# A mask built by VectorE instead of GpSimd, and a new list of steps, in a fused attention and feed-forward kernel

## The chip, the cores and the metric

The kernel runs on one core of one Trainium2 chip. A core has five engines with queues of their own: TensorE (PE) multiplies matrices, VectorE (DVE), ScalarE (ACT) and GpSimd (POOL) work on elements, and SyncE (SP) issues the DMAs. Each engine takes its instructions strictly in the order of its queue and waits at the head of it for semaphores of the others. The metric is the device time of one execution in microseconds; lower is better.

## The reference

For each of 32 heads (4 batches, 8 heads, head size 48, 768 time steps) a matrix state is decayed by a complex number per row, receives an outer product, and is read by the query. The 384 values of a token then pass a feed-forward layer with a gate.

```
mag = sqrt(a_re^2 + a_im^2);  scale = min(mag, 0.999) / (mag + 1e-6)
a_re_n, a_im_n = a_re*scale, a_im*scale
for t in range(768):
    new_re = a_re_n[t]*S_re - a_im_n[t]*S_im
    new_im = a_re_n[t]*S_im + a_im_n[t]*S_re
    S_re, S_im = new_re + outer(k[t], v[t]), new_im
    y[t] = q[t] @ S_re
x = y as (3072 tokens, 384);  h = x @ w_in (384 x 2048)
out = (h * sigmoid(1.702*h)) @ w_out (2048 x 384)
```

## The kernel before

The recurrence is done in chunks. The 3072 tokens are 12 units of 256 time steps, each of two chunks of 128. For a unit, `prepare` turns the decays into running products (scans on VectorE) and angles (logarithms, exponentials, arctangent, sine and cosine on ScalarE, whose function tables are reloaded between the kinds), and multiplies queries and keys by them: the last two multiplications are the rotations `rot0` (into tile `qr`) and `rot1` (in place in `qk`), line 231. The first unit is prepared in two halves of 128 steps, so that TensorE can start earlier. `remap` (L452 to L456) then copies the rotated data with ten DMAs per half into `qkh`, where the features of a head lie on the partitions. `attend` computes scores (L517), multiplies them by the causal mask (L523, result `pm`), turns the keys (L536), forms the new state (L561) and blends scores and state into the attention output (L507).

`moe` is the feed-forward layer. Its steps are a hidden product (L657), two SiLU passes on ScalarE (L669, L671) with a difference on VectorE (L673, `gl`), and an output product (L686). The units fall into seven groups; the first has one unit and works with whole fp32 weights (`valA0` to `valA7` of w_in, `valU0` to `valU7` of w_out), the others with weights split in a high and a low half (`hiA`, `loA`, ...). The weights arrive as 64-bit words. A weight tile is converted by four instructions: L249, L252 and L256 on VectorE and L255 on ScalarE; later it is split by L269 (ScalarE) and L274 (VectorE). Lines 718 to 743 check the ranges of weights and angles.

The mask has four blocks of 128 columns. Block 0 is made by a memset and an affine select; blocks 1 to 3 are block 0 with its four quarters of 32 partitions rotated, which takes twelve copies of 32 partitions x 128 columns (L160).

Every step of `prepare`, `attend`, `moe` and the conversions is entered in a `Plan` by `add`, with its engine and with what it reads and writes. The 1736 steps are then issued in the order of a table of numbers, `ORDER`, which sets the order in every engine's queue. The instructions ahead of the plan (constants, mask) are placed by the framework. Twenty products with the identity (L434, `WARM = 20`), whose result nobody reads, are steps as well; they wait for the first half's `rot1` and stand between TensorE's first steps. They write a bank that the first hidden product overwrites.

Of the kernel before, what the change touches and what calls it, by code (L numbers as in the profile page):

```python
# [16 lines left out]
ALU = mybir.AluOpType  # L17
# [78 lines left out]
def attention_moe(ctx: ExitStack, tc: tile.TileContext, qk_in, v, a_in, w_in, w_out, qn, kn, vn, an, bn, out):  # L96
# [49 lines left out]
    nc.vector.memset(b_hpi, HALF_PI)  # L146
    make_identity(nc, ident)
    nc.gpsimd.memset(mask, 1.0)
    nc.gpsimd.memset(runs, 1)
    run_of = {T: runs[:, 0 : NR * (T + 1)], L: runs[:, NR * (T + 1) :]}  # L150
    for n, x in run_of.items():
        nc.gpsimd.memset(x.rearrange("p (r t) -> p r t", t=n + 1)[:, :, 0], 0)
    nc.gpsimd.affine_select(
        out=mask[:, 0, :], in_=mask[:, 0, :], pattern=[[1, P]], compare_op=ALU.is_ge,
        fill=0.0, base=0, channel_multiplier=-1,
    )
    for j in range(1, 4):
        for g in range(4):
            o = (g + j) % 4
            nc.gpsimd.tensor_copy(out=mask[o * QL : (o + 1) * QL, j, :], in_=mask[g * QL : (g + 1) * QL, 0, :])  # L160
# [986 lines left out]
```

## Time and profile before

| | before |
|---|---|
| median of 3 runs | 550.34 us (550.18 to 550.40) |
| profiled execution | 550.39 us |
| its span in the trace | 548.7 us |
| TensorE busy | 521.2 us (95%) |
| VectorE busy | 391.1 us (71%) |
| ScalarE busy | 368.7 us (67%) |
| GpSimd busy | 12.3 us (2%) |

The span is what the trace covers; the time around it belongs to starting and ending the program. A busy engine is one with an instruction under way: two instructions of one engine overlap by some hundredths of a microsecond, so the time that one costs its queue is read from the start of the next.

### The profile page before, as it was taken

What the parts mean: (1) busy time and instruction counts of PE and PEld (TensorE: products, weight loads), DVE (VectorE), ACT (ScalarE), POOL (GpSimd) and SP (SyncE); (2) the same over time, 40 slices, a digit from 0 to 9 for tenths busy, and PEclk for the clock granted to TensorE, in tenths of its full rate; (3) what the DMA queues carried; (4) which work ended last, traced back from release to release, by engine and by line L of the source; (5) the groups of instructions that cost most, each with busy time, mean ns of one, the idle gap of its engine ahead of it and who ended that gap; (6) DMA issues with size and microseconds to landing.
All of it is one profiled execution on the core that took longest, in us unless ns stands there. A gap on an engine that the chain in (4) does not pass through costs nothing.

```text
span 548.7 us, 14354 instructions
## 1 busy us (share of the span) xinstructions
PE 521.2 (95%) x6122; PEld 446.9 (81%) x6122; DVE 391.1 (71%) x625; ACT 368.7 (67%) x559; POOL 12.3 (2%) x55
## 2 busy tenths in 40 slices
PE   0399999999999999999999999999999999999997
PEld 0389988999988888888888888888888888888885
DVE  7999999999979989987766844856366535421142
ACT  7898989979699988688795679248665242132221
POOL 7000000000000000000000000000000000000000
PEclk9999999999999999999999999999999999999999
DMA  8859963626576668868237427445441162100121
GB/s 344 284 191 354 252 258 89 206 54 156 201 181 202 151 197 206 236 168 252 74 92 228 68 65 174 145 133 117 136 134 49 50 145 91 62 15 34 39 87 61
DMA packets 29253, 82.02 MB, mean 149 GB/s; under 512 B 4096, under 2 KB 7168, under 8 KB 29184
## 3 DMA queue, kind: packets, MB, share of 16 engines
q1 hardware_dynamic: 29184, 81.06, 50.5%
q8 instruction: 49, 0.80, 0.6%
q14 instruction: 20, 0.16, 0.1%
HBM read 57.41 MB, written 4.72 MB: 113 GB/s over the span
## 4 chain that ended last, share of the span: by engine, by line
PE 89%; DVE 8%; DMA 1%; issue 1%; ACT 1%; SPq 0%; DVEq 0%
PE o_ps L686 36%; PE h_ps L657 36%; PE x_ps L507 7%; PE z_ps L561 3%; PE z_ps L517 3%; PE p_ps L517 2%; DVE qk L231 1%; PE p_ps L536 1%; PE z_ps L536 1%; DMA raw<-in_w_in_dram 1%; DVE s L231 1%; DVE valA L256 1%; DVE qr L231 1%; DVE valU L252 0%; DMA qkh<-qk 0%
## 5 line engine op out<-in xcount | busy, mean ns | idle before, releaser
L669 ACT ACTIVATE gh<-h_ps 128x512 fp32r<-128x512 f32 x88 | 52.4, 596 | 108.2 <-PE h_ps L657 76.5
L673 DVE TENSOR_TENSOR gl<-h_ps,gh 128x512 fp32r<-128x512 f32 x88 | 60.3, 687 | 85.3 <-ACT h_ps L671 74.0
L657 PE MATMUL h_ps<-xhi,hiA 128*128 128x512 f32 (+1 forms) x288 | 108.9, 378 | 0.4 <-DVE gl L673 0.4
L657 PE MATMUL h_ps<-xhi,loA 128*128 128x512 f32 (+1 forms) x288 | 107.1, 372 | 0.0
L657 PE MATMUL h_ps<-xlo,hiA 128*128 128x512 f32 (+1 forms) x288 | 107.0, 372 | 0.0
L686 PE MATMUL o_ps<-gh,hiU 128*128 128x512 f32 (+1 forms) x288 | 79.7, 377 | 0.0
L686 PE MATMUL o_ps<-gl,hiU 128*128 128x512 f32 (+1 forms) x288 | 79.4, 376 | 0.0
L686 PE MATMUL o_ps<-gh,loU 128*128 128x512 f32 (+1 forms) x288 | 78.2, 372 | 0.0
L890 ACT ACT_TABLE_LOAD x56 | 71.8, 1283 | 1.8 <-PEq L1135 0.9
L657 PEld LDWEIGHTS h_ps<-xhi,hiA 128*128 128x128 f32 x288 | 54.2, 188 | 10.6 <-DVE gl L673 0.9
L657 PEld LDWEIGHTS h_ps<-xhi,loA 128*128 128x128 f32 x288 | 54.2, 188 | 9.6
L657 PEld LDWEIGHTS h_ps<-xlo,hiA 128*128 128x128 f32 x288 | 54.3, 188 | 9.0
L686 PEld LDWEIGHTS o_ps<-gh,loU 128*128 128x128 f32 x288 | 52.3, 188 | 9.5
L686 PEld LDWEIGHTS o_ps<-gh,hiU 128*128 128x128 f32 x288 | 51.4, 188 | 9.9 <-ACT gh L669 0.5
L686 PEld LDWEIGHTS o_ps<-gl,hiU 128*128 128x128 f32 x288 | 51.5, 188 | 9.6 <-issue 0.4
L671 ACT ACTIVATE h_ps<-h_ps 128x512 f32<-128x512 f32 x88 | 51.8, 592 | 0.0
L231 DVE TENSOR_TENSOR qk<-qk,s 128x768 f32<-128x768 f32 (+2 forms) x39 | 44.0, 1134 | 0.8 <-ACT s L427 0.5
L507 PE MATMUL x_ps<-pm,v 128*32 128x128 f32 x768 | 39.4, 274 | 0.0
L723 DVE TENSOR_REDUCE fit<-raw_w 128x1 f32<-128x384 f32 x64 | 33.5, 544 | 5.4 <-DMA raw_w<-in_w_out_dram 4.4
L507 PE MATMUL x_ps<-qkh,st 96*32 96x128 f32 x640 | 34.0, 272 | 0.0
L434 PE MATMUL h_ps<-qk,ident 128*128 128x256 f32 x40 | 11.9, 460 | 22.2 <-DVE qk L231 22.2
L434 PEld LDWEIGHTS h_ps<-qk,ident 128*128 128x128 f32 x40 | 9.2, 237 | 23.8 <-issue 22.2
(104 smaller groups left out, 791.2 us busy)
## 6 DMA issues: line engine op xcount, KB each, us to landing
v<-in_v_dram SPq DMA_DIRECT2D x24, 416.0 KB, 4.4
ri<-in_a_dram SPq DMA_DIRECT2D x11, 768.0 KB, 5.9
qk<-in_qk_dram SPq DMA_DIRECT2D x11, 768.0 KB, 6.4
qkh<-qr SPq DMA_DIRECT2D x22, 288.6 KB, 5.8
qkh<-qk SPq DMA_DIRECT2D x22, 288.6 KB, 4.8
raw<-in_w_in_dram SPq DMA_DIRECT2D x8, 768.0 KB, 7.1
raw<-in_w_out_dram SPq DMA_DIRECT2D x8, 768.0 KB, 7.4
raw_w<-in_w_in_dram SPq DMA_DIRECT2D x16, 384.0 KB, 3.3
```

Source lines behind the costliest of these rows:

```text
L231: add(en, t, rank, lambda: e.tensor_tensor(out=out, in0=a, in1=b, op=alu), **kw)
L434: add("PE", 0.43, -WARM + k, lambda k=k, dst=dst: mm(h_ps[0][:, k % 2 * T : (k % 2 + 1) * T], lhsT=ident, rhs=dst[:, k % NR, 0:T], start=T ...
L507: mm(x_ps[32 * j : 32 * j + 32, r, :], lhsT=lt, rhs=rt, start=n == 0, stop=n == len(steps) - 1)
L517: mm(ps_[to : to + QL, j, lo:L], lhsT=at(h, 1, c)[:, lo : lo + QL], rhs=at(h, 0, c)[:, lo:L], start=True, stop=True)
L561: mm(z_ps[g * QL : (g + 1) * QL, h * D : h * D + D], lhsT=kt[h // 4][:, h % 4, g * QL : (g + 1) * QL], rhs=vt[:, lo : lo + D], start=True, ...
L657: mm(h_ps[hb][:, k * n_x : (k + 1) * n_x], lhsT=ww[:, r * T + f * P : r * T + (f + 1) * P], rhs=x[:, r, xs], start=n == 0, stop=n == last)
L669: add("ACT", a_t(CW) - 0.13, rk(order_), lambda hb=hb, gb=gb: act(out=high.g(gb), in_=h_ps[hb], func=AF.Silu, scale=SLOPE), r=[f"h{hb}"], ...
L671: add("ACT", a_t(CW) - 0.13, rk(order_), lambda hb=hb: act(out=h_ps[hb], in_=h_ps[hb], func=AF.Silu, scale=SLOPE), w=[f"h{hb}"], tab=SILU, ...
L673: add("DVE", d_t(CW), rk(order_), lambda hb=hb, gb=gb: dve.tensor_tensor(out=glo[gb], in0=h_ps[hb], in1=high.g(gb).bitcast(F32), op=ALU.su ...
L686: mm(o_ps[c][:, xs], lhsT=y[:, f * DM + c * P : f * DM + (c + 1) * P], rhs=x[:, k * n_x : (k + 1) * n_x], start=begins and k == 0 and n == ...
L723: add("DVE", d_t(CK), rk + 2, lambda x=x, op=op: dve.tensor_reduce(out=f_w[:, x, n : n + 1], in_=weights.looked_at()[:, :, 1], op=op, axis ...
L890: nc.scalar.preload_act_table_set(o[5])
```

## The change

The twelve copies of the mask are issued to VectorE, and block 0 of the mask is made first on GpSimd, ahead of the identity matrix and of the other constants; its memset covers 128 columns in place of 512. `ORDER` holds the same 1736 steps in another order, which concerns all engines from the first load to the last output. The steps themselves are the same.

```diff
+    nc.gpsimd.memset(mask[:, 0, :], 1.0)
+    nc.gpsimd.affine_select(
+        out=mask[:, 0, :], in_=mask[:, 0, :], pattern=[[1, P]], compare_op=ALU.is_ge,
+        fill=0.0, base=0, channel_multiplier=-1,
+    )
     make_identity(nc, ident)
-    nc.gpsimd.memset(mask, 1.0)
     nc.gpsimd.memset(runs, 1)
...
-    nc.gpsimd.affine_select(
-        out=mask[:, 0, :], in_=mask[:, 0, :], pattern=[[1, P]], compare_op=ALU.is_ge,
-        fill=0.0, base=0, channel_multiplier=-1,
-    )
     for j in range(1, 4):
         for g in range(4):
             o = (g + j) % 4
-            nc.gpsimd.tensor_copy(out=mask[o * QL : (o + 1) * QL, j, :], in_=mask[g * QL : (g + 1) * QL, 0, :])
+            nc.vector.tensor_copy(out=mask[o * QL : (o + 1) * QL, j, :], in_=mask[g * QL : (g + 1) * QL, 0, :])
...
 ORDER = """
-80 0 137 5 15 20 100 25 81 82 84 83 85 86 1 3 2 87 94 139 4 138 88 103
```

On VectorE's queue, in the first unit's first half (`s0` to `s4` are its work tiles), the instructions behind the first ratio stood so before:

```order
L231 TENSOR_TENSOR s1_84<-ri_80,s3_86 128x3x128
L256 ISA valA0_159<-raw0_72,valA0_159 128x1536
L231 TENSOR_TENSOR s1_84<-s0_83,s1_84 128x3x128
L249 TENSOR_SCALAR valA1_173<-raw1_73 128x768
L339 TENSOR_SCALAR s0_83<-s0_83 128x3x128
L252 SCALAR_TENSOR_TENSOR valA1_173<-raw1_73,valA1_173 128x768
L358 SCALAR_TENSOR_TENSOR s3_86<-s0_83,s2_85 128x129 x3
L231 TENSOR_TENSOR s1_84<-ri_80,s3_86 128x3x128
```

and stand so now:

```order
L231 TENSOR_TENSOR s1_84<-ri_80,s3_86 128x3x128
L160 COPY mask_64<-mask_64 32x128 x12
L249 TENSOR_SCALAR valA1_166<-raw1_73 128x768
L339 TENSOR_SCALAR s0_83<-s0_83 128x3x128
L252 SCALAR_TENSOR_TENSOR valA1_166<-raw1_73,valA1_166 128x768
L256 ISA valA0_158<-raw0_72,valA0_158 128x1536
L231 TENSOR_TENSOR s1_84<-s0_83,s1_84 128x3x128
L358 SCALAR_TENSOR_TENSOR s3_86<-s0_83,s2_85 128x129 x3
L231 TENSOR_TENSOR s1_84<-ri_80,s3_86 128x3x128
```

The twelve copies stand behind the first half's ratio (the first row), and the last conversion step of `valA0` (L256) and the second half's sum (the next L231) have moved behind the conversion of `valA1`.

On TensorE's queue the first instructions were:

```order
L434 MATMUL h_ps0_107<-qk_81,ident_63 128x256 x13
L536 MATMUL o_ps0_109<-ident_63,qkh0_78 128x96 x4
L517 MATMUL p_ps_104<-qkh0_78 32x128 x4
L517 MATMUL p_ps_104<-qkh0_78 32x96 x4
L517 MATMUL p_ps_104<-qkh0_78 32x64 x4
L517 MATMUL p_ps_104<-qkh0_78 32x32 x4
L517 MATMUL z_ps_105<-qkh0_78 32x128 x4
L517 MATMUL z_ps_105<-qkh0_78 32x96 x4
L517 MATMUL z_ps_105<-qkh0_78 32x64 x4
L517 MATMUL z_ps_105<-qkh0_78 32x32 x4
L434 MATMUL h_ps0_107<-qk_81,ident_63 128x256 x5
L536 MATMUL o_ps1_110<-ident_63,qkh0_78 128x96 x4
```

and are:

```order
L434 MATMUL h_ps0_107<-qk_81,ident_63 128x256 x11
L536 MATMUL o_ps0_109<-ident_63,qkh0_78 128x96 x4
L434 MATMUL h_ps0_107<-qk_81,ident_63 128x256
L517 MATMUL z_ps_105<-qkh0_78 32x128 x4
L517 MATMUL z_ps_105<-qkh0_78 32x96 x4
L517 MATMUL z_ps_105<-qkh0_78 32x64 x4
L517 MATMUL z_ps_105<-qkh0_78 32x32 x4
L517 MATMUL p_ps_104<-qkh0_78 32x128 x4
L517 MATMUL p_ps_104<-qkh0_78 32x96 x4
L517 MATMUL p_ps_104<-qkh0_78 32x64 x4
L517 MATMUL p_ps_104<-qkh0_78 32x32 x4
L536 MATMUL o_ps1_110<-ident_63,qkh0_78 128x96 x4
```

Eleven instead of thirteen of the products with the identity stand ahead of the first useful one; one stands behind it, the two halves of the scores have changed places, and the five ahead of the second key turn are gone from there. Both queues hold all twenty of them ahead of the first hidden product or between the steps up to it.

On VectorE's queue the last two conversions of w_out, `valU6` and `valU7`, had this between them:

```order
L256 ISA valU6_893<-raw2_74,valU6_893 128x1536
L571 TENSOR_TENSOR xlo1_94<-x_ps_106,xhi1_886 128x3x128
L231 TENSOR_TENSOR qk_81<-qk_81,s3_86 128x3x256
L523 TENSOR_TENSOR pm1_98<-z_ps_105,mask_64 128x512
L231 TENSOR_TENSOR qk_81<-qk_81,s2_85 128x3x256
L249 TENSOR_SCALAR valU7_945<-raw3_75 128x768
L231 TENSOR_TENSOR qr_82<-qk_81,s0_83 128x3x512
L252 SCALAR_TENSOR_TENSOR valU7_945<-raw3_75,valU7_945 128x768
L231 TENSOR_TENSOR s1_84<-s3_86,s1_84 128x3x256
L274 TENSOR_TENSOR loA0_1012<-valA0_159,hiA0_226 128x768
L256 ISA valU7_945<-raw3_75,valU7_945 128x1536
```

and have now:

```order
L256 ISA valU6_835<-raw2_74,valU6_835 128x1536
L523 TENSOR_TENSOR pm1_98<-z_ps_105,mask_64 128x512
L523 TENSOR_TENSOR pm0_97<-p_ps_104,mask_64 128x512
L231 TENSOR_TENSOR qk_81<-qk_81,s2_85 128x3x256
L571 TENSOR_TENSOR xlo1_94<-x_ps_106,xhi1_935 128x3x128
L252 SCALAR_TENSOR_TENSOR valU7_858<-raw3_75,valU7_858 128x768
L231 TENSOR_TENSOR qr_82<-qk_81,s0_83 128x3x512
L256 ISA valU7_858<-raw3_75,valU7_858 128x1536
```

The split of `valA0` (L274) and the next unit's sum no longer stand between the two, and two mask products do.

## Rows read from the trace of the kernel before

**Rows 1.** The page, part 1: busy us, share of the span and instructions of each engine

```profile
PE 521.2 (95%) x6122; PEld 446.9 (81%) x6122; DVE 391.1 (71%) x625; ACT 368.7 (67%) x559; POOL 12.3 (2%) x55
```

**Rows 2.** Waits of TensorE over the span: us in total, times, longest

```profile
PE h_ps L434 <- DVE qk L231: 22.2, 1, 22.2
PE z_ps L561 <- DVE pm L523: 0.8, 1, 0.8
PE h_ps L657 <- DVE gl L673: 0.4, 1, 0.4
```

**Rows 3.** TensorE in time: start us, us, line, tiles, records, idle before and releaser

```profile
22.21 8.38 PE L434 MATMUL h_ps<-qk,ident 128*128 128x256 f32 x26 [22.21 <-DVE qk L231]
30.43 0.49 PE L536 MATMUL o_ps<-ident,qkh 96*128 96x96 f32 x4
...
32.10 2.43 PE L434 MATMUL h_ps<-qk,ident 128*128 128x256 f32 x10
...
37.45 0.84 PE L561 MATMUL z_ps<-v,kt 128*32 128x48 f32 x46 [0.78 <-DVE pm L523]
...
39.92 2.94 PE L657 MATMUL h_ps<-x,valA 128*128 128x128 f32 x24
...
86.16 1.56 PE L657 MATMUL h_ps<-x,valA 128*128 128x256 f32 x6
87.56 0.49 PE L536 MATMUL p_ps<-ident,qkh 96*128 96x96 f32 x4
...
88.22 1.49 PE L686 MATMUL o_ps<-g,valU 128*128 128x256 f32 x6
...
92.21 4.18 PE L686 MATMUL o_ps<-g,valU 128*128 128x256 f32 x18
96.05 0.47 PE L657 MATMUL h_ps<-xhi,hiA 128*128 128x256 f32 x1
```

**Rows 4.** Busy us in stretches: PE, PEld, DVE, ACT, POOL, PEclk, DMA share, GB/s

```profile
10.00:20.00 10.00, 0.00 (x0) 0.00 (x0) 9.96 (x24) 8.65 (x16) 0.99 (x6) 1.00 1.03 412
...
90.00:100.00 10.00, 10.00 (x152) 9.22 (x142) 9.96 (x15) 9.56 (x12) 0.00 (x0) 1.00 0.71 150
```

**Rows 5.** Tile valU, 84 to 97 us: duration ns, starts; idle us caused, times

```profile
L256 DVE CUSTOM_DVE_ANT_0 valU<-raw,valU x2: 948/948/949, 83.9 to 92.5; 128x1536 uint16<-128x1536 uint16 x2
...
  DVE valU L256: 0.2, 1
```

**Rows 6.** VectorE in time, columns as for TensorE above

```profile
5.19 0.56 DVE L231 TENSOR_TENSOR s<-s,s 128x384 f32<-128x384 f32 x1 [2.40 <-ACT s L207]
...
7.66 0.64 DVE L231 TENSOR_TENSOR s<-ri,s 128x384 f32<-128x384 f32 x1
8.23 1.04 DVE L256 CUSTOM_DVE_ANT_0 valA<-raw,valA 128x1536 uint16<-128x1536 uint16 x1
...
10.32 0.77 DVE L339 TENSOR_SCALAR s<-s 128x384 f32<-128x384 f32 x1
...
12.84 0.53 DVE L231 TENSOR_TENSOR s<-ri,s 128x384 f32<-128x384 f32 x1
13.29 0.15 DVE L366 TENSOR_SCALAR small<-s 128x3 f32<-128x3 f32 x1
...
13.57 0.53 DVE L249 TENSOR_SCALAR valA<-raw 128x768 int32<-128x768 int32 x1
14.02 0.42 DVE L339 TENSOR_SCALAR s<-s 128x384 f32<-128x384 f32 x1
...
15.49 0.53 DVE L231 TENSOR_TENSOR qk<-qk,s 128x384 f32<-128x384 f32 x1
...
21.15 0.96 DVE L231 TENSOR_TENSOR qk<-qk,s 128x768 f32<-128x768 f32 x1
...
36.61 0.69 DVE L523 TENSOR_TENSOR pm<-z_ps,mask 128x512 f32<-128x512 f32 x1
```

**Rows 7.** GpSimd in time, 3 to 11 us

```profile
3.64 6.34 POOL L160 COPY mask<-mask 32x128 bf16<-32x128 bf16 x12
```

145 rows, old and new, of the table ORDER are left out of this document.

## The prediction

> **What bounds the kernel now.** I read the page's busy shares first: TensorE is busy for 521.2 of 548.7 us [rows 1]. The waits of TensorE come next [rows 2]: one of 22.2 us ahead of its first instruction, one of 0.8 and one of 0.4. The rest of its idle time lies behind its last product. From 22 us on the kernel is a TensorE queue that hardly ever stops, so a change that adds and removes no useful product can gain at the start, at those two waits, and nowhere else; it can lose anywhere.
>
> The start is read from TensorE in time [rows 3]. The first thing that it does, at 22.21, is the run of 26 records of identity products (13 products, two records each). They do no useful work; the first useful product is at 30.43, and another run of them at 32.10 is one of two that stand between useful steps (14 records in all). They wait for VectorE's `rot1`, which starts at 21.15 and takes 0.96 [rows 6]. So `rot1` sets when TensorE's queue starts, and the fillers, twenty before and after, only shift with it.
>
> VectorE sets `rot1`: it is busy for 9.96 of the 10 us from 10 to 20 [rows 4], so whatever is put ahead of `rot1` on its queue delays it. It stays the second bound up to about 96 us: from 90 to 100 it is busy 9.96 of 10 us, and the tile `valU7`, ready at 92.5 + 0.95 = 93.45, made TensorE's weight load wait 0.2 us [rows 4, 5]. TensorE then starts the second group's first hidden product at 96.05 [rows 3]. Behind that TensorE waited for VectorE once more, 0.4 us at L657 [rows 2].
>
> **The change part by part.** *The copies.* VectorE is idle for 2.40 us ahead of 5.19, where it waits for ScalarE's squares [rows 6]. By the order of its queue the copies do not run there: they stand behind the ratio (7.66 before), in the stretch without idle time. The queue is in order, so all twelve are paid by `rot1`. The trace has no such copy on VectorE. From below: an operation on 3 columns takes 0.15 us and hides 0.08 of it under its neighbour (12.84 + 0.53 = 13.37 against a start at 13.29), net 0.07, twelve of them 0.84. From above: one on 384 fp32 columns takes 0.42, twelve of them 5.0 [rows 6]. At 128 columns the straight line between the two is 0.15 + 0.27 x 125/381 = 0.24, less 0.08 = 0.16; the elements are half as long, so I take 0.13, or 1.56 us.
>
> [...]
>
> *What GpSimd gives back.* Its twelve copies ran from 3.64 for 6.34 us [rows 7]. In that time VectorE was slower than later on the same shapes [rows 6]: L231 0.64 against 0.53, twice; L256 1.04 against 0.95 [rows 5]; L339 0.77 against 0.42. That is 0.11 + 0.11 + 0.09 + 0.35 = 0.66 us, which `rot1` gets back. GpSimd's queue has little else that anybody needs early.
>
> [...]
>
> *The new order ahead of `rot1`.* The same instructions stand ahead of it in both, but for one more L249 (five weight tiles begun, not four). That is 14.02 - 13.57 = 0.45 us [rows 6]. SP now puts one more weight of 768 KB ahead of the first load of `qk`. At 412 GB/s [rows 4] that is 1.9 us; its first user stood at 15.49 [rows 6] and stands some four instructions later, so this is hidden. Without that cover it would cost up to 1.9.
>
> `rot1` therefore ends 1.56 + 0.45 - 0.66 = 1.35 us later, and TensorE's queue with it.
>
> *What TensorE gets back.* The wait of 0.78 us at 37.45 [rows 3] was for `pm`, whose second half VectorE did at 36.61 [rows 6], behind five conversion steps. In the new queue both halves of `pm` follow the second half's `rot1` directly. Five fillers stand behind the blend, so the hidden products' input is ready too. I take the 0.78 as gone. What is late next is the second half: its `rot1` has moved back behind two conversions and a sum, about 2.6 us at 0.87 each. TensorE asks for it later as well: six hidden products now stand ahead of the second chunk's scores.
>
> *The conversions.* Two tiles decide. Ahead of `valU7` the new queue lacks a split and a sum (0.87 each net, as 0.95 less 0.08) and has the copies: 93.45 - 1.74 + 1.56 - 0.66 = 92.6. TensorE asks for it 12 of the last 18 records (4.18 us) ahead of the second group [rows 3], about 2.6 us, so at 96.05 + 1.35 - 0.78 - 2.6 = 94.0: early. Ahead of `valU6` the queue gains the copies, an L249 and an L231 and lacks one mask product (0.69 - 0.08 = 0.61): 84.85 + 1.56 + 0.45 + 0.87 - 0.61 - 0.66 = 86.5. TensorE reaches it a key turn (two rows of 0.33 net) and three products of `valA7` (87.56 - 86.16 = 1.40) earlier than before: before, 96.05 - 88.22 = 7.83 ahead of the second group, now 7.83 + 0.66 + 1.40 = 9.89, so at 96.62 - 9.89 = 86.7 [rows 3, 5]. That is 0.2 us to spare, no more. A near miss of this kind cost 0.2 at `valU7`, so I add 0.2.
>
> *The rest.* Behind 100 us the useful products and the last three outputs are the same, in another order. I cost that at nothing: its cover is the slack of VectorE and ScalarE, which over the span are busy for 71% and 67% [rows 1], most of it early. The 0.4 at L657 [rows 2] may stay or go, and without that cover each missed product would cost TensorE about as much.
>
> **Sum.** 1.35 - 0.78 + 0.2 = +0.77 us on the profiled 550.39 (span 548.7 and 1.69 around it), or 551.16. The median was 0.05 below the profiled execution, so I predict 551.1, inside the 0.2% (1.1 us) that a measurement of this kernel can tell from no change.
>
> **The rivals.** *Faster.* The copies cost 0.84, GpSimd's disturbance was larger than my four pairs show (the conversions between them and the scans behind them too, another 0.3), no near miss bites, and the 0.4 at L657 goes. Then 0.84 + 0.45 - 0.96 - 0.78 - 0.4 = -0.85, or 549.5; with the straight 1.0 us between products around the wait at 37.45 in place of 0.78, 549.3. For it: the copies have half-length elements. Against it: all of it has to come together, since the queue has no more to give.
>
> *Slower: VectorE takes the lead.* From a price of 0.15 a copy on, `valU6` comes after TensorE asks for it, and each further hundredth costs 0.12 at the start and moves that tile equally, with its place among mask products that themselves wait for TensorE's scores. At the line's 0.24 (nothing hidden), 12 x 0.11 = 1.3 us more, and two or three just-in-time tiles at 0.3 each: 551.16 + 1.3 + 0.7 = 553.2. For it: VectorE is full up to 100 us [rows 4]. Against it: the elements are short.
>
> *Slower: the check loads at the end.* In the new queue a range check that waits for its own load stands ahead of a `gl` once more than before. If TensorE's output product comes first, it waits about 0.5: 551.7. For it: loads take microseconds. Against it: the 0.4 at L657 is the only such wait in the whole trace.
>
> *The change does not do what it says.* That the copies fill idle time is already taken as false. If they did, 1.56 would go and the time be 549.6.
>
> **How the numbers follow.** My forecast with its neighbours (549.3 to 551.4) has 0.45. Faster has 0.2, of which the part below 549.25, a gain that can be told, is 0.17; VectorE in the lead 0.25; the check loads and other new waits behind 100 us 0.1. Of the last two and of the forecast's upper edge, 0.39 lies above 551.45. What is left, 0.44, is within 0.2%. The range leaves out a tenth on either side: 549.3 from the first rival, 553.2 from the second.
>
> **What would show it.** Right: twelve copies near 8 us on VectorE of about 0.2 us each and 1.6 in all; L339 at about 0.42 at once; TensorE's first record near 23.5; no wait for `pm` near 36; the second group's first hidden product near 96.8. Wrong: TensorE's first record before 22.5 (copies cheap or hidden), a wait for `valU6` above 0.5, the second group before 96, or a wait above 1 us anywhere behind 100 us.

## The result: 0.77% slower, outside the predicted range

The changed kernel takes 554.3 us (median of 4 runs, 554.07 to 555.54), the kernel before 550.29 beside it; the ratio is 1.0077 [1.0064, 1.0090]. Predicted were 551.1 us and a range from 549.3 to 553.2. The profiled execution is the longest of the four (555.54); what is its own is told apart below.

The page of the changed kernel, part 1, answers to [rows 1]:

```profile
PE 522.9 (94%) x6122; PEld 446.4 (81%) x6122; DVE 392.5 (71%) x637; ACT 369.8 (67%) x560; POOL 5.4 (1%) x43
```

TensorE's waits in the changed kernel, as in [rows 2] (total us, times, longest):

```profile
PE h_ps L434 <- DVE small L366: 24.4, 1, 24.4
PE h_ps L657 <- DVE xlo L571: 0.8, 1, 0.8
PE o_ps L686 <- ACT gh L669: 0.6, 1, 0.6
PE z_ps L561 <- DMA v<-in_v_dram: 0.5, 1, 0.5
PE o_ps L686 <- DVE osb L703: 0.3, 1, 0.3
```

The first has grown from 22.2 us, those for pm and `gl` are gone, and four others stand in their place. (The releaser named in the first row is merely the last semaphore; the tile is `rot1`'s: it ends at 24.27, 0.10 ahead of TensorE's first record, as it did before.) TensorE in time, answering to [rows 3]:

```profile
24.37 7.80 PE L434 MATMUL h_ps<-qk,ident 128*128 128x256 f32 x22 [24.37 <-DVE small L366]
32.01 0.50 PE L536 MATMUL o_ps<-ident,qkh 96*128 96x96 f32 x4
...
36.10 0.88 PE L561 MATMUL z_ps<-v,kt 128*32 128x48 f32 x48 [0.51 <-DMA v<-in_v_dram]
...
98.33 0.47 PE L657 MATMUL h_ps<-xhi,hiA 128*128 128x256 f32 x1
```

The start is 2.16 us later (24.37 against 22.21), the second group 2.28 later (98.33 against 96.05). From there to the last product's start it is 451.1 us against 448.4. So 2.2 us are lost at the start, nothing is won up to the second group, and 2.7 are lost behind it. In the other runs of this list the loss behind it is 1.5 to 2.1, in list_only (below) 1.8; what is above that belongs to this one execution. VectorE in time in the changed kernel, answering to [rows 6], with two stretches behind 100 us:

```profile
7.44 0.55 DVE L231 TENSOR_TENSOR s<-ri,s 128x384 f32<-128x384 f32 x1
8.01 2.38 DVE L160 COPY mask<-mask 32x128 bf16<-32x128 bf16 x12
10.42 0.56 DVE L249 TENSOR_SCALAR valA<-raw 128x768 int32<-128x768 int32 x1
10.90 0.42 DVE L339 TENSOR_SCALAR s<-s 128x384 f32<-128x384 f32 x1
...
23.31 0.96 DVE L231 TENSOR_TENSOR qk<-qk,s 128x768 f32<-128x768 f32 x1
...
152.94 1.01 DVE L723 TENSOR_REDUCE fit<-raw_w 128x1 f32<-128x384 f32 x2
153.86 0.41 DVE L703 TENSOR_SCALAR osb<-o_ps 128x256 f32<-128x256 f32 x1
...
233.12 0.52 DVE L723 TENSOR_REDUCE fit<-raw_w 128x1 f32<-128x384 f32 x1
233.56 1.75 DVE L398 TENSOR_TENSOR_SCAN s<-runs,s 128x771 f32<-128x771 uint8 x1
235.22 0.53 DVE L571 TENSOR_TENSOR xlo<-x_ps,xhi 128x384 fp32r<-128x384 f32 x1
```

The twelve copies cost the queue 10.42 - 8.01 = 2.41 us, 0.20 each and none overlapped; L339 takes 0.42 at once, L231 0.55, so GpSimd's disturbance is gone as forecast; `rot1` starts at 23.31 instead of 21.15. Behind 100 us, `xlo` stands behind a scan of 1.75 us, and TensorE, which has nothing else to do in the meantime, waits 0.8 for it; the third `osb` stands behind two range checks.

### The profile page after: what moved, and what is told of

It reads as the page before. It is cut to its first block, busy times and chain, and to the rows that moved or that the text cites. A ratio compares the mean times of both kernels' runs of the same rounds, so it can differ in the third digit from the quotient of the medians.

```text
span 553.7 us, 14339 instructions
## 1 busy us (share of the span) xinstructions
PE 522.9 (94%) x6122; PEld 446.4 (81%) x6122; DVE 392.5 (71%) x637; ACT 369.8 (67%) x560; POOL 5.4 (1%) x43
## 4 chain that ended last, share of the span: by engine, by line
PE 52%; DMA 1%; ACT 1%; DVE 0%; SPq 0%; issue 0%; ACTq 0%
PE o_ps L686 23%; PE h_ps L657 22%; PE x_ps L507 4%; DMA ri<-in_a_dram 1%; PE z_ps L561 1%; PE z_ps L517 1%; PE p_ps L517 1%; PE p_ps L536 1%; PE z_ps L536 1%; ACT L890 0%; ACT s L207 0%; SPq L718 0%; ACT gh L669 0%; ACT s L331 0%; DVE osb L703 0%
## 5 line engine op out<-in xcount | busy, mean ns | idle before, releaser
L231 DVE TENSOR_TENSOR qk<-qk,s 128x768 f32<-128x768 f32 (+2 forms) x39 | 44.0, 1138 | 0.4
```

Of the source, the lines that this page charges most:

```text
L231: add(en, t, rank, lambda: e.tensor_tensor(out=out, in0=a, in1=b, op=alu), **kw)
```

## The experiments

The ratio is to the kernel before, in runs on the same chip, given as a 95% interval. It reaches 0.5 to 0.8 us to either side, so the times of two runs that lie less than 0.7 to 1 us apart do not tell them from each other. *Start* is TensorE's first record, *group 2* the first product of the second group, *rest* the time from there to the start of the last product, all three of the profiled execution, which can differ from the median by up to 1.2 us. copy_prices, copy_prices_apart and copy_partitions are not in the table: each is one execution, read for the price of a copy alone.

| run | median us | ratio | start | group 2 | rest |
|---|---|---|---|---|---|
| before | 550.3 | | 22.21 | 96.05 | 448.4 |
| changed | 554.3 | [1.0064, 1.0090] | 24.37 | 98.33 | 451.1 |
| mask_only | 552.12 | [1.0019, 1.0043] | 24.00 | 97.79 | 448.5 |
| list_only | 551.91 | [1.0024, 1.0051] | 22.18 | 95.72 | 450.2 |
| copies_first_new | 553.18 | [1.0041, 1.0068] | 23.04 | 96.78 | 450.5 |
| copies_first_old | 550.40 | [0.9992, 1.0010] | 22.25 | 96.03 | 448.6 |
| st_not_on_gpsimd | 551.93 | [1.0015, 1.0039] | 21.85 | 96.54 | 448.5 |
| v_early | 554.70 | [1.0068, 1.0096] | 24.62 | 98.21 | 450.3 |
| late_waits | 553.70 | [1.0046, 1.0073] | 24.41 | 98.53 | 449.8 |
| own_tile | 554.88 | [1.0065, 1.0092] | 24.47 | 98.55 | 450.5 |
| new_opening_old_rest | 550.11 | [0.9991, 1.0009] | 23.06 | 96.72 | 448.2 |
| old_opening_new_rest | 553.32 | [1.0040, 1.0067] | 22.17 | 95.97 | 452.2 |
| mask_by_selects | 549.84 | [0.9984, 1.0002] | 21.65 | 95.46 | 449.1 |
| best_mix | 550.16 | [0.9987, 1.0005] | 22.21 | 95.38 | 448.3 |
| selects_two_steps | 549.74 | [0.9980, 0.9998] | 21.57 | 95.22 | 448.7 |

### The two halves of the change

**mask_only** is the changed kernel with the `ORDER` of before.

> The table of the kernel before, with the mask's copies on VectorE as in the change. Theory (both parts cost: the copies are paid in full by VectorE, the list costs the rest): twelve copies at 0.20 one behind the other, 2.41 us, less 0.66 for GpSimd's disturbance, so TensorE's first record at 22.21 + 1.75 = 23.96 and the time 550.3 + 1.75 = 552.0; the wait of 0.8 for pm stays, the waits behind 100 us don't come. Rival A (the list alone is at fault, the copies are hidden): 550.3 or below, first record at 22.2 or before. Rival B (the copies alone are at fault, everything later follows from VectorE's lateness): 554.3.

**list_only** is the kernel before with the `ORDER` of the change.

> The table of the change, with the mask's copies on GpSimd as before. Theory: the start pays only for one more L249, 0.45, first record near 22.7; the waits behind 100 us (xlo L571, gh L669) are the list's own and stay: 554.3 - 1.75 = 552.5. Rival A (the list alone): 554.3. Rival B (the copies alone, the list harmless): 550.3 + 0.45 - 0.8 for the wait for pm = 550.0.

TensorE in time in list_only:

```profile
22.18 6.93 PE L434 MATMUL h_ps<-qk,ident 128*128 128x256 f32 x22 [22.18 <-DVE small L366]
...
33.49 0.88 PE L561 MATMUL z_ps<-v,kt 128*32 128x48 f32 x48 [0.95 <-DMA v<-in_v_dram]
...
95.72 0.47 PE L657 MATMUL h_ps<-xhi,hiA 128*128 128x256 f32 x1
```

Both parts cost. The mask costs 1.8, all at the start (24.00 - 22.21 = 1.79, where 2.41 - 0.66 = 1.75 was expected), and nothing later: the rest takes 448.5. The list costs 1.6: nothing at the start, where I expected 0.45, a gain of 0.3 up to group 2, and 1.8 behind it. Together that is 3.3 of the 4.0 us. The L249 that I charged 0.45 for was balanced, since in the new order other instructions meet GpSimd's copies: L339 takes 0.51 in list_only, not 0.77 as in [rows 6].

VectorE in time in list_only:

```profile
8.62 0.51 DVE L339 TENSOR_SCALAR s<-s 128x384 f32<-128x384 f32 x1
```

So the copies gain less from GpSimd's silence there: with them the start moves by 24.37 - 22.18 = 2.19, not 1.79. The list's free start is that of this execution: the same opening, also with the mask on GpSimd, starts at 23.06 in new_opening_old_rest (below).

### Are the copies free in idle time?

**copies_first_new** and **copies_first_old** (the new and the old list):

```diff
-    for j in range(1, 4):
-        for g in range(4):
+    def turn_mask():
+        for j, g in [(j, g) for j in range(1, 4) for g in range(4)]:
...
+        turn_mask()
         for n in order:
```

> The table of the change, with the twelve copies put at the head of VectorE's queue, ahead of the first sum (L231, 5.1 us), where VectorE waits for ScalarE's squares. Theory: block 0 of the mask is there at 1.5 us, VectorE is free from 2.8, so the copies run to 5.2 and delay the first sum by 0.1; the start gets back 2.3 of 2.41 us: first record at 22.1, time 554.3 - 2.3 = 552.0. Rival A (the start does not matter, the later waits set the end): 554 or above. Rival B (later waits grow out of VectorE's lateness at the start and go with it): 550 or below.

> The table of the kernel before, with the twelve copies on VectorE at the head of its queue. Theory: GpSimd's disturbance of 0.66 us goes, the first sum is 0.1 late, so TensorE's first record moves from 22.21 to 21.65 and the time from 550.3 to 549.7. Rival (the half microsecond is lost again at a later wait, for pm or for the first converted weights): 550.3. Rival (the copies in the idle time delay the first sum by more than 0.6): above 550.4.

Both missed, by 1.2 and 0.7 us; the start came 0.9 and 0.6 late. VectorE in copies_first_old:

```profile
2.80 3.22 DVE L160 COPY mask<-mask 32x128 bf16<-32x128 bf16 x12
6.05 0.56 DVE L231 TENSOR_TENSOR s<-s,s 128x384 f32<-128x384 f32 x1
```

GpSimd in copies_first_old:

```profile
2.66 0.47 POOL L163 MEMSET st<- 128x448 f32 x1
...
3.14 0.47 POOL L163 MEMSET st<- 128x448 f32 x1
...
3.68 0.10 POOL L342 MEMSET s<- 128x3 f32 x1
```

The copies take 3.22 us, not 2.4: the first one alone lasts 1.02 and ends at 3.83, when GpSimd's last memset is done (3.78). The first sum slips from 5.19 to 6.05 [rows 6]. copies_first_new shows the same, with copies of 3.21 us and the sum at 6.04. **st_not_on_gpsimd** takes the two memsets of 0.47 away from GpSimd:

```diff
-    for x in st:
-        nc.gpsimd.memset(x, 0.0)
+    def clear_st():
+        for x in st: nc.vector.memset(x, 0.0)
...
+            if n == 170:
+                clear_st()
```

> As copies_first_old, but the two memsets of st (0.47 us each, 2.67 to 3.62 on GpSimd) are done by VectorE at about 25 us. In copies_first_old the first copy lasted 1.02 us, from 2.81 to 3.83, and GpSimd's last memset ended at 3.78. Theory (a bf16 copy of VectorE stands still while GpSimd is at work): GpSimd is now done at about 3.1, the first copy ends there, the twelfth at 5.3, the first sum starts at 5.3 instead of 6.05 and TensorE at 21.7; time near 550.0, with 0.5 for the memsets later on. Rival (the first copy is long by itself, as the first of its kind): it again lasts 1.0, first sum at 6.05, TensorE at 22.2.

VectorE in st_not_on_gpsimd:

```profile
2.80 2.39 DVE L160 COPY mask<-mask 32x128 bf16<-32x128 bf16 x12
5.26 0.56 DVE L231 TENSOR_TENSOR s<-s,s 128x384 f32<-128x384 f32 x1
```

The theory holds: the first copy takes 0.20, the sum starts at 5.26 and TensorE at 21.85. The time does not follow (551.93, expected near 550.0): the wait for pm grew from 0.4 us in copies_first_old to 1.4, since VectorE now does the memsets ahead of it, for 0.83 us from 30.06. That accounts for the profiled execution (551.05); what the median has above it, another 0.9, no trace shows. In copies_first_old the first copy, from 2.80 on, ran beside several of GpSimd's memsets (two of 0.47 and seven small ones) and ended 0.05 behind the last; by what mechanism it was held no run shows.

### What is a copy worth?

**copy_prices** and **copy_prices_apart** put copies of several forms into the changed kernel at about 21 us, into a tile not yet in use; the second gives each a place of its own.

> The changed kernel with 30 more instructions on VectorE behind its 27th (at about 18 us), into a tile that is not yet in use, five of each form: the mask's copy of 32 x 128 bf16 to other partitions; the same to the same partitions; 128 x 128 bf16; 32 x 64 fp32 (the same bytes); 32 x 128 fp32; and the 32 x 128 bf16 copy written as a multiplication by 1. Wanted: which of them starts the next one 0.08 us before its own end, as the fp32 instructions of the trace do. Theory A (bf16 copies, being short, do not overlap): the three bf16 copies 0.20 apart, the fp32 copies and the multiplication 0.08 less than they last. Theory B (copies to other partitions do not overlap): the second and third forms 0.12 apart. Theory C (an instruction that reads or writes the tile of the one before does not overlap): all six 0.2 or more apart. The time is not compared; it is some 6 us longer.

> In copy_prices all six forms cost 0.22 to 0.25 each, and each waited for the one before, because all wrote the same place. Here four of each of five forms on VectorE, each to a place of its own, so that none waits for the one before: the mask's copy of 32 x 128 bf16 into another tile; 32 x 128 fp32; the bf16 copy written as a multiplication by 1; the fp32 one as a multiplication by 1; and 128 x 128 bf16. Theory A (bf16 copies do not overlap with their neighbours, whatever they write): 0.19 to 0.20 apart for bf16, the fp32 forms 0.08 less than they last, about 0.13. Theory B (copies do not overlap, multiplications do): 0.20 for the copies, 0.12 for both multiplications. Theory C (reading and writing one tile was what kept the mask's copies apart): all five 0.11 to 0.14 apart. The time is not compared; it is some 4 us longer.

```diff
+                a, f, t = mask[:, 0, :], ident, osb_all.rearrange("p a b -> p (a b)")
+                b, u, w = t.bitcast(BF16), pm[0].rearrange("p a b -> p (a b)"), pm[1].rearrange("p a b -> p (a b)").bitcast(BF16)
+                for x in range(4):
+                    nc.vector.tensor_copy(out=b[32:64, x * P : (x + 1) * P], in_=a[0:32, :])
+                for x in range(4):
+                    nc.vector.tensor_copy(out=t[32:64, 320 + x * P : 448 + x * P], in_=f[0:32, :])
...
```

In copy_prices every form was 0.22 to 0.25 us apart, 0.03 behind the end of the one before, which had written the same place; it told nothing but the durations (0.18 for 32 x 128 bf16, 0.22 for fp32). VectorE in copy_prices_apart, in the order of the expectation:

```profile
20.94 0.49 DVE L893 COPY osb<-mask 32x128 bf16<-32x128 bf16 x4
21.36 0.61 DVE L895 COPY osb<-ident 32x128 f32<-32x128 f32 x4
21.90 0.48 DVE L897 TENSOR_SCALAR osb<-mask 32x128 bf16<-32x128 bf16 x4
22.31 0.62 DVE L899 TENSOR_SCALAR pm<-ident 32x128 f32<-32x128 f32 x4
22.94 0.50 DVE L901 COPY pm<-mask 128x128 bf16<-128x128 bf16 x4
```

Four bf16 copies take 0.49 us, so they start 0.10 apart and last 0.18: half of the price in the mask. It looked like theory C, so **own_tile** lets the mask's copies read block 0 from another tile:

```diff
+    tri = sb.tile([P, P], BF16, name="tri")
...
-            nc.vector.tensor_copy(out=mask[o * QL : (o + 1) * QL, j, :], in_=mask[g * QL : (g + 1) * QL, 0, :])
+            nc.vector.tensor_copy(out=mask[o * QL : (o + 1) * QL, j, :], in_=tri[g * QL : (g + 1) * QL, :])
```

> The changed kernel with block 0 of the mask made once more in a tile of its own (one more memset and select on GpSimd), from which the twelve copies on VectorE read; places and lists are those of the change. Theory (what kept the copies 0.20 apart was that they read and wrote one tile): twelve copies 0.10 apart, 1.2 us instead of 2.41, TensorE's first record at 23.2 and the time 554.3 - 1.2 = 553.1. Rival (in this place they stay 0.20 apart): 554.3. Rival (the start gained is lost at the wait for v or for pm, as in v_early): copies 0.10 apart, but 554 or above.

VectorE in own_tile:

```profile
8.11 2.38 DVE L160 COPY mask<-tri 32x128 bf16<-32x128 bf16 x12
```

Theory C fell: again 2.38 us, and the time stayed (554.88). What the mask's copies do and the others did not is to change partitions with every copy. **copy_partitions** separates that:

> own_tile left the twelve copies 0.20 apart, so reading and writing one tile is not what keeps them apart. In copy_prices_apart all copies of a form read the same 32 partitions and wrote the same 32, and were 0.10 apart; the one place without overlap was the step from 32 partitions to 128. The mask's copies change their partitions with every copy. Here, on VectorE at about 20 us in the changed kernel, 20 copies of 32 x 128 bf16 into places of their own, four of each kind: same partitions read and written; same read, written ones alternate; read ones alternate, same written; both alternate, as in the mask; and 32 and 128 partitions in turn. Theory D (an instruction on other partitions than the one before does not overlap with it): 0.10 apart in the first kind, 0.20 in the fourth and fifth, and the second and third tell which side counts. Rival (it is something else of the place near 8 us, such as the DMA traffic of 315 to 412 GB/s there): 0.10 in all. The time is not compared.

```diff
+                for x in range(4):
+                    nc.vector.tensor_copy(out=col(x)[32:64], in_=a[0:32])
+                for x in range(4, 8):
+                    nc.vector.tensor_copy(out=col(x)[32 + x % 2 * 32 : 64 + x % 2 * 32], in_=a[0:32])
...
+                for x in range(16, 20):
+                    nc.vector.tensor_copy(out=col(x)[0 : 32 + x % 2 * 96], in_=a[0 : 32 + x % 2 * 96])
```

VectorE in copy_partitions, four copies a row: same partitions; written ones alternate; read ones alternate; both; 32 and 128 partitions in turn, from partition 0:

```profile
20.94 0.49 DVE L893 COPY osb<-mask 32x128 bf16<-32x128 bf16 x4
21.35 0.78 DVE L895 COPY osb<-mask 32x128 bf16<-32x128 bf16 x4
22.05 0.78 DVE L897 COPY osb<-mask 32x128 bf16<-32x128 bf16 x4
22.84 0.78 DVE L899 COPY osb<-mask 32x128 bf16<-32x128 bf16 x4
23.63 0.49 DVE L901 COPY osb<-mask 32x128 bf16<-32x128 bf16 x4
```

Theory D holds, with one correction: where the partition at which a copy starts to read or to write differed from the copy before, it started only behind that one's end, 0.20 apart, against 0.10 in the first row; whether it covered 32 or 128 partitions made no difference (fifth row, 0.49 for four as in the first). The rival falls too: these copies are 0.20 apart at 21 us, far from the place near 8. Each of the twelve copies of the mask starts to read and to write at other partitions than the one before, as those of the fourth row do, and I had not allowed for it.

### What the list costs behind 100 us

**new_opening_old_rest** (the mask on GpSimd) and **old_opening_new_rest** cut the table at the second group's first hidden product: the steps ahead of it in one table, then those that are left in the order of the other.

> The mask on GpSimd as before; the table of the change up to the first hidden product of the second group (98 us), and from there the steps that are left in the old table's order. Theory: what the list costs stands behind 100 us, in its own order of VectorE's and ScalarE's queues, so the rest takes the old 448.4 us instead of 450.2: first product near 22.2, second group at 95.7, time 550.1. Rival (the new opening leaves VectorE or the checks behind, and the waits come from that): 551.9, as with the whole new list.

> The change's mask on VectorE; the old table up to the second group, and from there the steps that are left in the new table's order. Theory (the new order behind 100 us costs 1.8 whatever stands ahead): first record at 24.0 and second group at 97.8 as in mask_only, the rest 450.2 instead of 448.4, time 552.1 + 1.8 = 553.9. Rival (the new rest is slow only behind the new opening): 552.1.

The first came out at 550.11 with a rest of 448.2: the 1.8 us of list_only come from the order of the rest. It started at 23.06, not 22.2, and TensorE waited 1.24 us ahead of the product with v, so the total says less than the rest does. The late start is VectorE's wait for a weight that the new list wants earlier; VectorE in new_opening_old_rest:

```profile
8.62 0.70 DVE L249 TENSOR_SCALAR valA<-raw 128x768 int32<-128x768 int32 x1 [0.52 <-DMA raw<-in_w_in_dram]
9.24 0.77 DVE L339 TENSOR_SCALAR s<-s 128x384 f32<-128x384 f32 x1
```

In list_only, with the same opening, this L249 started at 8.06 without a wait, and L339 behind it met less of GpSimd's copies (0.51). In the changed kernel the mask's copies stand ahead of it. So with the mask on GpSimd the new opening can wait for a load, as it did in one of three profiled executions (list_only, this one, best_mix).

The second ran with the mask on GpSimd as before, other than its expectation says; by the same reasoning theory then gives 22.2, 96.05 and 552.1, the rival 550.3. It took 553.32: the new order of the rest costs behind the old opening too, and by these numbers more (rest 452.2 in the profile, of an execution 0.8 above the median). TensorE's waits in old_opening_new_rest:

```profile
PE o_ps L686 <- ACT gh L669: 1.7, 2, 0.9
PE z_ps L561 <- DVE pm L523: 0.9, 1, 0.9
PE h_ps L657 <- DVE xlo L571: 0.8, 1, 0.8
```

**late_waits** moves two steps of the changed kernel's list on VectorE:

```diff
-L723 TENSOR_REDUCE fit<-raw_w 128x1 x2
 L703 TENSOR_SCALAR osb<-o_ps_109 128x256
+L723 TENSOR_REDUCE fit<-raw_w 128x1 x2
...
+L571 TENSOR_TENSOR xlo_94<-x_ps,xhi_935 128x3x128
 L398 SCALAR_TENSOR_TENSOR s_87<-runs,s_84 128x771
-L571 TENSOR_TENSOR xlo_94<-x_ps,xhi_935 128x3x128
```

> The changed kernel with two steps of VectorE's list moved: xlo (L571, 235.2 us) ahead of the 1.75 us scan (L398) that stands before it, and the third osb (L703, 153.9 us) ahead of two range checks (L723). Theory: the two waits of TensorE that the trace shows there, 0.92 and 0.46 above the usual distance, go: 554.3 - 1.4 = 552.9. Rival (TensorE waits at the next place for something else, ScalarE's chain behind the later scan for one): 554.3 or above.

Expected were 552.9, measured 553.7; by the intervals neither the full gain nor none is excluded. Both waits are gone, and the rest takes 449.8 us, 0.4 less than in list_only, but a new wait has come, 9 us behind `xlo`; TensorE in late_waits:

```profile
244.20 0.76 PE L517 MATMUL z_ps<-qkh 96*32 96x128 f32 x32 [0.44 <-ACT st L581]
```

**v_early** moves the two loads of v on SP's queue:

```diff
 L326 DMA ri<-in_a_dram 128x1536
+L615 DMA v_88<-in_v_dram 128x832
+L615 DMA v_89<-in_v_dram 128x832
 L452 DMA qkh_78<-qr 48x768 x2
...
 L456 DMA qkh_78<-qr 16x256 x2
-L615 DMA v_89<-in_v_dram 128x832
-L615 DMA v_88<-in_v_dram 128x832
```

> The changed kernel with the first two loads of v (L615) ahead of the remap's DMAs on SP's queue, at about 15 us instead of 29.9. Theory: TensorE's wait of 0.5 us for v at 36.1 (0.65 above the usual distance of the two products) goes and nothing takes its place: 554.3 - 0.65 = 553.6. Rival (pm or the second half's remap comes only just after v, so another wait takes its place): 554.3. Rival (the loads of v take time from the loads of weights and qk at 412 GB/s, 0.84 MB or 2 us): up to 555.

The time shows no gain (554.70, not told from the changed kernel's), as the rivals have it. In the traces, start to group 2 takes 73.6 us instead of 74.0, but the start lies 0.25 later, so group 2 comes 0.12 earlier. TensorE in v_early:

```profile
35.54 0.88 PE L561 MATMUL z_ps<-v,kt 128*32 128x48 f32 x48 [0.27 <-DVE pm L523]
...
93.13 0.43 PE L507 MATMUL x_ps<-pm,v 128*32 128x128 f32 x8 [0.37 <-DMA v<-in_v_dram]
```

The first v is in time, pm comes just behind it, and the next unit's v is late at 93.13.

### Versions that might beat both

**mask_by_selects** (old list):

```diff
-        for g in range(4):
-            o = (g + j) % 4
-            nc.gpsimd.tensor_copy(out=mask[o * QL : (o + 1) * QL, j, :], in_=mask[g * QL : (g + 1) * QL, 0, :])
+        for rows, base in ((P, j * QL), (j * QL, j * QL - P)):
+            m = mask[0:rows, j, :]
+            nc.gpsimd.affine_select(out=m, in_=m, pattern=[[1, P]], compare_op=ALU.is_ge, fill=0.0, base=base, channel_multiplier=-1)
```

> The kernel before, with the twelve copies of the mask replaced by six affine selects on GpSimd that make blocks 1 to 3 in place (0.29 us each by the trace, against 0.53 for a copy). Theory: GpSimd is done at about 5.5 us instead of 10, VectorE is disturbed only there, and the 0.66 us come back: first product at 21.6, time 549.7. Rival (ScalarE sets the start as soon as VectorE is earlier, as with the copies at the head of the queue): first product at 22.2, time 550.3. Rival (the selects disturb VectorE more than copies): above 550.5.

GpSimd in mask_by_selects:

```profile
3.06 1.26 POOL L160 TENSOR_SCALAR_AFFINE_SELECT mask<-mask 128x128 bf16<-128x128 bf16 x5
...
5.46 0.09 POOL L342 MEMSET s<- 128x3 f32 x1
```

GpSimd is done at 5.5, the start is 21.65, the median 549.84, all as expected, though the interval reaches 1, so a gain in time is not shown. **best_mix** puts v_early's opening ahead of it, **selects_two_steps** moves pm and gl on VectorE:

```diff
+L523 TENSOR_TENSOR pm_98<-z_ps,mask 128x512
 L256 ISA valU_205<-raw_76,valU_205 128x1536
-L523 TENSOR_TENSOR pm_98<-z_ps,mask 128x512
...
+L673 TENSOR_TENSOR gl_102<-h_ps_108,gh_1108 128x512
 L339 TENSOR_SCALAR s_86<-s_86 128x3x256
-L673 TENSOR_TENSOR gl_102<-h_ps_108,gh_1108 128x512
```

> The mask by six affine selects on GpSimd; the new table up to the second group with the first two loads of v ahead of the remap; the rest in the old table's order. Theory: the two gains add up, 0.4 of the selects and 0.3 to 0.6 of the new opening now that v comes in time: second group at 95.0, the rest 448.3, time 549.4. Rival (VectorE sets the second group, so the wait for v is paid again at a later weight or mask tile): 549.8, as with the selects alone. Rival (the new opening's one more load of 768 KB ahead of qk makes the start depend on when loads land): 550.1 with a wide spread.

> mask_by_selects with two steps of the old table moved on VectorE: the second pm (L523, 36.6 us) ahead of one conversion step (L256), and gl (L673, 105.7) ahead of L339. Theory: TensorE's waits for them, 0.78 and 0.35 by the trace (1.0 and 0.54 above the usual distance), shrink by 0.8 and 0.5: 549.85 - 1.3 = 548.5. Rival (VectorE sets the second group, so what is gained at pm is lost at a weight tile): 549.3, gl's 0.5 alone. Rival (both are lost again): 549.8.

best_mix gave 550.16, with an interval that covers the selects' 549.84. Its profile has the shortest time up to group 2 from the start (73.2 us against 73.8), but its start lay at 22.21, 0.56 behind the selects'. The trace says why: five L249 stand ahead of `rot1` in the new opening and four in the old, as the prediction had counted, and the first sum starts 0.11 later (5.21 against 5.10). The fifth L249 costs the queue 20.09 - 19.62 = 0.47 us; VectorE in best_mix:

```profile
19.62 0.55 DVE L249 TENSOR_SCALAR valA<-raw 128x768 int32<-128x768 int32 x1
20.09 0.95 DVE L231 TENSOR_TENSOR qr<-qk,s 128x768 f32<-128x768 f32 x1
```

selects_two_steps has the lowest median, 549.74 [0.9980, 0.9998], below the kernel before by little and not told from the selects alone (549.84). Both waits went, but of the 1.3 us expected 0.1 arrived. Group 2 came only 0.24 earlier, and a new wait of 0.3 us, for ScalarE's `g` (L665), stands at 55.9.

## Why the prediction was wrong

The miss is 3.2 us. Three terms of the sum make it up: the rest, costed at nothing, is 1.8; the twelve copies are 0.85; from the start to group 2 it is 0.7 in the profiled execution, and between 0.3 and 0.9 in the other runs of this list in the table.

- *The place of the copies, GpSimd's 0.66, the direction:* right. The copies ran from 8.01 and were paid in full by `rot1`; the shapes that GpSimd had slowed were back at once; the start moved by 2.41 + 0.45 - 0.66 = 2.20 by measured terms, 2.16 by the trace.
- *The price of a copy, 0.13 or 1.56 us for twelve:* mis-sized. A copy lasted 0.19, near the 0.21 behind my 0.13 (0.13 + 0.08), but I had deducted 0.08 for the overlap that the fp32 rows show [rows 6]. Those rows all start at partition 0; the copies change it each time, and none overlaps: they are 0.20 apart, as in the rows of copy_partitions that change it. 0.85 us of the miss. That half-length elements shorten a copy is shown: 0.18 us for 32 x 128 in bf16 against 0.22 in fp32 (copy_prices).
- *"I take the 0.78 as gone", with hidden products' input "ready too":* the wait for pm went, and one for v (0.51, and 0.95 in list_only) took its place. I counted SP's load of a weight, not that v (L615) had moved behind the first half's whole remap: it was issued at 25.68 before and at 29.86 now, 6.2 us ahead of its use at 36.10. From the start to group 2 I expected 0.58 less; it became 0.12 more. v_early says that little was to be had there: pm and the next v stood right behind.

SyncE's queue before, and then in the changed kernel:

```profile
25.68 0.59 SPq L615 DMA_DIRECT2D v<-in_v_dram  x1
```

```profile
29.86 1.05 SPq L615 DMA_DIRECT2D v<-in_v_dram  x2
```

- *The near miss at `valU6`:* no wait there, nor at another weight. 0.2 too much.
- *"The rest. I cost that at nothing", covered by VectorE's 71% and ScalarE's 67%:* the step that failed worst. The rest takes 1.8 us more in list_only. A busy share says nothing of what stands ahead of one instruction: `xlo` stood behind a scan of 1.75 us, while VectorE had idle time enough elsewhere, and TensorE waited 0.8 for it. VectorE kept to the order of its list (the mask's copies ran at their place, from 8.01, though copies_first_new has them start at 2.80), and I read the order of the two queues only up to 97 us. The profiled execution adds some 0.9; its wait of 0.6 for `gh`, near 261 us, is not in list_only with the same list. That the order of the rest costs the 1.8 is shown, since the old order behind the same opening takes them back (new_opening_old_rest, 448.2); which of its instructions cost it is open: late_waits took two waits away, and its gain of 0.6 is within the intervals.
- *The rivals:* "VectorE takes the lead" had the price above 0.15 right and 553.2 near, but its just-in-time weight tiles did not wait. The check loads at the end were not it: checks stood ahead, but of `osb`, at 154 (a load of theirs took 3.4 us from issue to landing, by the page of the changed kernel). The time lies 1.1 above the range, less than the rest's 1.8. The prediction's own sign, a wait above 1 us behind 100 us, did not show: TensorE's waits there are 0.8 and less.

Still open: which of the other differences in the order make up what late_waits and v_early did not bring back.

## What to carry to other kernels

On VectorE a copy's price depended on its neighbour: 0.20 us where the starting partition changed from one copy to the next, 0.10 where it did not (copy_partitions), so no overlap may be deducted for the first kind. When a table reorders all queues, read what now stands ahead of each tile that TensorE asks for, to the end of the span and on SyncE too; average idle time does not cover it (VectorE was busy for 71% of the span, and TensorE waited 0.8 us for `xlo`). A wait taken away is worth only the distance to the next one: of 1.3 us expected, 0.1 came back in selects_two_steps, with a new wait in its trace; in late_waits and v_early, too, another wait came close behind, though there the times are too near to say how much was lost.

## What the runs showed of the hardware

A bf16 copy of 32 x 128 on VectorE costs 0.10 us behind one with the same starting partitions and 0.20 behind one with others (copy_partitions). Covering 128 partitions did not change the first (0.49 us for four, as with 32), nor reading another tile the second (2.38 us for twelve in own_tile). Such a copy that met GpSimd's memsets lasted 1.02 us in copies_first_old and ended 0.05 behind the last of them; with the two of 0.47 us taken from GpSimd it lasted 0.20 (st_not_on_gpsimd). On GpSimd a select of 128 x 128 takes 0.29 us (mask_by_selects), its copies 0.53 each on the mean [rows 7] (0.44 in new_opening_old_rest, 5.26 us for twelve), so that six selects replace twelve copies in 1.5 us.
